# Loading a small vector last on SyncE's queue instead of first on ScalarE's

## The chip, the core and the metric

The kernel runs on one core of a Trainium2 chip. The core has a matrix engine (TensorE, "PE" in the profile, with its weight loads shown apart as "PEld"), a vector engine (VectorE, "DVE"), a scalar engine (ScalarE, "ACT"), GpSimd ("POOL") and SyncE ("SP"), which here only issues DMAs. ScalarE issues a few DMAs too. Every engine works through its own list of instructions in order, and waits on semaphores for what others produce. The metric is the device time of one execution in microseconds (us); what is compared is the median of several executions.

## What is computed

The reference is a state-space convolution block followed by a two-layer network. Shortened:

```python
# q, k, v: (1, 2048, 512) bf16; shift_k: (512, 4); ssm_k: (512, 2048); ssm_D: (512,)
k_shift = sum over t of k_pad[:, t:t + S, :] * shift_k[:, ks - 1 - t]
kv  = k_shift * v
y   = irfft(rfft(kv, 2 * S) * rfft(ssm_k, 2 * S))[:S] + kv * ssm_D    # along the sequence
h   = x + layernorm(x) * y                                            # x is q
out = h + relu(layernorm(h) @ w1) @ w2
```

What matters for this change is ssm_D, 512 numbers of 2 bytes. Since kv * ssm_D is the convolution of kv with a single tap at position 0, the kernel adds ssm_D to the real part of the spectrum of ssm_k, and needs nothing more of it.

## The kernel before

All is written for one core and these sizes, with the order of the instructions on each engine fixed by the order in the program text.

**Loads.** `wsh` (the four shift taps) is loaded on ScalarE's queue at L95. Right behind it, on the same queue, two loads bring ssm_D (L102, tile `d0`, in the trace "d"): one for each half of the 64 + 64 partitions. Each writes the same 64 columns of four row groups to all 64 partitions, so that each half is 64 partitions of 4 runs of 64 numbers, 32 KB. On SyncE's queue follow nine loads in this order: k of the first 512 tokens (a DMA transpose, L125, tile `kT`), all of ssm_k (a plain load of 2 MB, L122, into the tile `pre`), v of the first 512 tokens (a DMA transpose, L127, tiles `vT`), and then k and v in turns for the other three quarters. SyncE's next instruction after these is the load of x at L405, which can only start when the memory of the middle stage is free.

**First stage, to about 38 us.** TensorE runs eleven warm-up matmuls (L115), then the taps of the first quarter: `taps(u)` multiplies k by diagonal matrices (L273, tile `pkv` in PSUM), and `times_v(u)` on VectorE multiplies the result by v (L280, tile `kvx`). When ssm_k is there, 64 transposes (L219) bring it into rows, and eight groups of `stage1` (L246, copied out by ScalarE and VectorE at L233 and L235) make the first half of its spectrum. The taps of the later quarters stand between these groups.

**GpSimd in this stage.** It makes the negated table `cn` from `cs` in eight pieces (L211, in the trace "c2n"). Between the first and the second piece it copies ssm_D into the order in which it is used (L213, tile `dtab`, from "d"). It then clears `dre` and `dim` (L300, L301), and fills them by eight small operations from `dsc` ("dm_f" in the trace, L318). `dre` and `dim` are the matrices of the inverse transform at L455, which runs from about 94 us.

**Second stage, from about 38 us.** `kvx` is brought into rows (L219 again, tile `xfl`). Then the pool `early` is closed, which holds `d0`, `dsc`, `kvx` and some tables, and a pool is opened in its place which holds `kf`. `spectrum_k` makes the second half of the spectrum of ssm_k: matmuls (L261, L263, tile `ps2k`), then VectorE adds `dtab` to the real part on the way from PSUM to `kf` (L336), and ScalarE copies the imaginary part (L337). The first L336 is the first to need `dtab`, and the first to write over the memory of `early`.

**Later stages** (products, inverse transform, layer norms, the two-layer network and the stores, L367 to L596) use nothing of what is moved, but for `dre` and `dim`.

Of the kernel before, what the change touches and what calls it, by code (L numbers as in the profile page):

```python
# [15 lines left out]
P = 128  # L16
# [40 lines left out]
def kernel(  # L57
# [13 lines left out]
    nc = tc.nc  # L71
# [5 lines left out]
    DC = D // P  # L77
# [19 lines left out]
    pre = slotA.tile([P, 4096 + 2048], I32, tag="A", name="pre")  # L97
    skf = pre[:, 0:4096].bitcast(BF16)
    d0 = early.tile([P, DC, 64], BF16, name="d0")
    for dp in range(2):  # L100
        src = bass.AP(tensor=A_ssm_D.tensor, offset=A_ssm_D.offset + 64 * dp, ap=[[0, 64], [P, DC], [1, 64]])
        nc.scalar.dma_start(out=d0[64 * dp:64 * dp + 64, :, :], in_=src)  # L102
    CH = 512
    vTs = [vp.tile([P, DC, CH], BF16, name=f"vT{c}") for c in range(4)]
    kT = kvp.tile([P, DC, 16 + S], BF16, name="kT")
# [13 lines left out]
    for c, src in ((0, "k"), (0, "s"), (0, "v"), (1, "k"), (1, "v"), (2, "k"), (2, "v"), (3, "k"), (3, "v")):  # L119
        ts = slice(CH * c, CH * c + CH)  # L120
        if src == "s":
            nc.sync.dma_start(out=skf.rearrange("p (c t) -> p c t", c=DC),  # L122
                              in_=A_ssm_k.rearrange("(c p) t -> p c t", p=P))
        elif src == "k":
            nc.sync.dma_start_transpose(out=kT[:, :, 16 + CH * c:16 + CH * c + CH], in_=k_d[ts, :])  # L125
        else:
            nc.sync.dma_start_transpose(out=vTs[c][:], in_=v_d[ts, :])  # L127


    TURN = 2.0 * math.pi * SIN_SHRINK  # L130
# [46 lines left out]
    def table(dst, turns, dps=(0, 1)):  # L177
        for dp in dps:
            nc.scalar.activation(out=dst[:, :, 64 * dp:64 * dp + 64], in_=turns, func=ACT.Sin,  # L179
                                 scale=hsc[:, dp:dp + 1], bias=hbi[:, dp:dp + 1])  # L180
# [27 lines left out]
    dtab = consts.tile([P, 8, DC, 8], BF16, name="dtab")  # L208
    for h in range(8):
        hs = slice(4 * h, 4 * h + 4)  # L210
        nc.gpsimd.tensor_single_scalar(out=cn[:, hs, :], in_=cs[:, hs, :].bitcast(F32), scalar=-1.0, op=ALU.mult)  # L211
        if h == 0:
            nc.gpsimd.tensor_copy(out=dtab[:], in_=d0[:].rearrange("p r (o g) -> p o r g", g=8))  # L213


    def to_rows(cols, q, fl, eng):
# [52 lines left out]
    def taps(u):  # L269
        c, rg = divmod(u, DC)  # L270
        ps = psum.tile([P, CH], F32, tag="ps", name="pkv")
        for j in range(KS):
            nc.tensor.matmul(out=ps[:], lhsT=wdiag[:, rg, j, :], rhs=kT[:, rg, CH * c + 16 - j:CH * c + CH + 16 - j],  # L273
                             start=(j == 0), stop=(j == KS - 1))
        return u, ps

    def times_v(u, ps):
        c, rg = divmod(u, DC)
        split = "p (a h l) -> p a h l"
        nc.vector.tensor_tensor(out=kvx[:, :, rg, 8 * c:8 * c + 8, :].rearrange("p h a l -> p a h l"),  # L280
                                in0=ps[:].rearrange(split, h=16, l=4),
                                in1=vTs[c][:, rg, :].rearrange(split, h=16, l=4), op=ALU.mult)

    def group_k(gb):
        stage1(gb, kfl, lambda o, j, n: a1k[:, :, 32 * o + j:32 * o + j + n], "AADAAADA")
# [22 lines left out]
    for gb in range(8):  # L308
        for u in ((4, 5), (6,), (7,), (8, 9), (10, 11), (12,), (13, 14), (15,))[gb]:
            times_v(*taps(u))  # L310
        group_k(gb)
        if 2 <= gb < 6:

            hs = slice(8 * gb - 16, 8 * gb - 8)
            table(cc[:, hs], r2[:, hs], (1,))
    for pq in halves:
        for dst, rho, blk, sgn in ((dre, 0, 0, 1.0), (dre, 1, 1, 1.0), (dim, 0, 1, -1.0), (dim, 1, 0, 1.0)):
            nc.gpsimd.tensor_single_scalar(out=dst[pq, rho, pq], in_=dsc[pq, blk, :], scalar=sgn / 2048, op=ALU.mult)  # L318
# [367 lines left out]
```

## Time and profile before

| what | value |
|---|---|
| median of 5 executions | 218.05 us (217.62 to 219.07) |
| the profiled execution's own time | 219.07 us |
| its span in the trace | 217.3 us |
| mean granted clock of TensorE | 0.983 |
| ssm_D: two issues on ScalarE's queue, first and last start | 1.2 and 1.9 us |
| ssm_D: from issue to landing | 4.2 and 5.6 us |
| ssm_k: issue, time to landing | 2.19 us, 10.5 us |
| last issue of v on SyncE's queue: start, length, time to landing | 26.77 us, 2.30 us, 6.1 us |
| GpSimd: the eight operations of L318 | 26.27 to 29.35 us |
| first use of `dtab` (L336) | 42.58 us |

The span is the time from the first to the last instruction in the trace; the execution's own time is a little longer. Engines overlap, so their busy times don't add up to the span. Rows for a group of instructions give the engine, the operation, what is written and read, how many there are, how long they were busy, and what ended the idle time of the engine before them. For a DMA, "landing" is when its semaphore has been counted up, and "ACTq" and "SPq" are the engines that issue it; an issue takes the engine some time of its own. "q1" is the queue of SyncE's loads, "q10" that of ScalarE's, "q8" that by which instructions are loaded. The names of tiles lack their numbers.

### The profile page before, as it was taken

What the parts mean: (1) busy time and instruction counts of PE and PEld (TensorE: products, weight loads), DVE (VectorE), ACT (ScalarE), POOL (GpSimd) and SP (SyncE); (2) the same over time, 40 slices, a digit from 0 to 9 for tenths busy, and PEclk for the clock granted to TensorE, in tenths of its full rate; (3) what the DMA queues carried; (4) which work ended last, traced back from release to release, by engine and by line L of the source; (5) the groups of instructions that cost most, each with busy time, mean ns of one, the idle gap of its engine ahead of it and who ended that gap; (6) DMA issues with size and microseconds to landing.
All of it is one profiled execution on the core that took longest, in us unless ns stands there. A gap on an engine that the chain in (4) does not pass through costs nothing.

```text
span 217.3 us, 7312 instructions
## 1 busy us (share of the span) xinstructions
PE 204.3 (94%) x3129; PEld 141.4 (65%) x3129; DVE 147.2 (68%) x300; ACT 125.8 (58%) x240; POOL 67.7 (31%) x103
## 2 busy tenths in 40 slices
PE   7969888999999999999986999999999999999993
PEld 2466444999989999979973778554454544444442
DVE  6976877989989998867977779742973167130032
ACT  2485797798888888868935389103650337106500
POOL 6049930000019999978221120210022002000000
PEclk9999999999999999999998599999999999999999
DMA  6999980000000000049990000332124110621012
GB/s 129 354 200 147 186 165 8 0 8 3 3 3 3 2 3 0 0 113 223 278 298 4 6 3 0 51 69 55 27 50 63 39 50 0 91 73 32 0 42 54
DMA packets 30383, 15.40 MB, mean 71 GB/s; under 512 B 25520, under 2 KB 29072, under 8 KB 30224
## 3 DMA queue, kind: packets, MB, share of 16 engines
q1 hardware_dynamic: 28992, 14.75, 31.1%
q8 instruction: 24, 0.39, 0.8%
q10 hardware_dynamic: 1360, 0.20, 0.6%
q14 instruction: 7, 0.06, 0.1%
HBM read 7.08 MB, written 2.10 MB: 42 GB/s over the span
## 4 chain that ended last, share of the span: by engine, by line
PE 78%; SPq 6%; DVE 5%; DMA 3%; issue 3%; ACT 2%; DVEq 0%
PE ps2m L591 18%; PE ps1m L579 16%; PE pz L511 10%; PE psy L386 7%; SPq L127 4%; PE ps L246 4%; PE pkv L273 4%; PE psi L455 4%; PE u L261 4%; PE ps2k L261 4%; PE u L263 4%; DMA vT<-in_A_v_dram 3%; PE ps2k L263 3%; PE pst L219 2%; SPq L125 2%
## 5 line engine op out<-in xcount | busy, mean ns | idle before, releaser
L581 ACT ACTIVATE h1T<-ps1m 128x512 bf16<-128x512 f32 (+3 forms) x55 | 27.4, 514 | 25.9 <-PE ps1m L579 25.1
L579 PE MATMUL ps1m<-hlnT,w 128*128 128x512 bf16 (+3 forms) x220 | 39.6, 337 | 0.3
L591 PE MATMUL ps2m<-w,h1T 128*128 128x512 bf16 (+3 forms) x187 | 39.1, 367 | 0.0
L593 DVE TENSOR_TENSOR o<-ps2m,xh 128x512 bf16<-128x512 f32 (+1 forms) x17 | 11.1, 659 | 37.6 <-PE ps2m L591 37.1
L579 PEld LDWEIGHTS <-w 128*128 128x128 bf16 (+1 forms) x220 | 21.8, 100 | 17.6 <-issue 1.4
L591 PEld LDWEIGHTS <-h1T 128*128 128x128 bf16 (+1 forms) x187 | 17.9, 98 | 20.6 <-issue 1.6
L511 PE MATMUL pz<-bp,ecore 32*32 32x128 f32 x1024 | 22.2, 388 | 2.6 <-issue 2.0
L233 ACT CAST a<-ps 128x512 fp32r<-128x512 f32 x40 | 21.1, 593 | 4.4 <-PE ps L246 2.9
L525 POOL TENSOR_SCALAR rstd<-mv 128x4 f32<-128x4 f32 (+1 forms) x9 | 2.1, 230 | 67.2 <-DVE mv L532 61.3
L520 ACT CAST zt<-pz 128x512 bf16<-128x512 f32 x16 | 8.4, 596 | 24.6 <-PE pz L511 21.6
L511 PEld LDWEIGHTS pz<-bp,ecore 32*32 32x32 f32 x1024 | 15.6, 110 | 8.3 <-issue 4.6
L376 POOL TENSOR_TENSOR t<-usb,kf 128x320 fp32r<-128x320 f32 x22 | 19.7, 943 | 1.7 <-ACT usb L367 1.6
L376 DVE TENSOR_TENSOR t<-u,kf 128x704 fp32r<-128x704 f32 x22 | 18.4, 883 | 1.8 <-ACT usb L367 1.6
L233 ACT CAST kf<-psy 128x512 fp32r<-128x512 f32 x30 | 17.6, 647 | 1.9 <-PE psy L386 0.2
L530 DVE BATCH_NORM_STATS2 st<-xh 128x6 f32<-128x512 bf16 x28 | 17.3, 678 | 0.0
L235 DVE CAST a<-ps 128x512 fp32r<-128x512 f32 x24 | 15.8, 686 | 1.9 <-PE ps L246 1.8
L455 PE MATMUL psi<-dre,kf 128*128 128x256 f32 x64 | 15.2, 285 | 0.2 <-ACT kf L233 0.2
L273 PE MATMUL pkv<-kT,wdiag 128*128 128x512 bf16 x64 | 15.4, 381 | 0.0
L455 PE MATMUL psi<-dim,kf 128*128 128x256 f32 x64 | 15.1, 285 | 0.0
L211 POOL TENSOR_SCALAR c2n<-c2s 128x512 fp32r<-128x512 f32 x8 | 11.8, 1513 | 9.1 <-ACT c2s L179 9.1
L280 DVE TENSOR_TENSOR kvx<-pkv,vT 128x512 bf16<-128x512 f32 x16 | 10.5, 686 | 5.4 <-DMA vT<-in_A_v_dram 4.8
L455 PEld LDWEIGHTS psi<-dre,kf 128*128 128x128 f32 x64 | 12.1, 192 | 0.7 <-ACT kf L233 0.7
(119 smaller groups left out, 400.4 us busy)
## 6 DMA issues: line engine op xcount, KB each, us to landing
pre<-in_A_ssm_k_dram SPq DMA_DIRECT2D x1, 2048.0 KB, 10.5
out_dram<-o SPq DMA_DIRECT2D x58, 32.0 KB, 1.6
xh<-in_A_q_dram SPq DMA_DIRECT2D x4, 384.0 KB, 7.0
w<-in_B_w_dram SPq DMA_DIRECT2D x1, 1376.0 KB, 12.7
w<-in_B_w_dram SPq DMA_DIRECT2D x1, 1280.0 KB, 16.0
xh<-in_A_q_dram SPq DMA_DIRECT2D x4, 128.0 KB, 3.1
hlnT<-hln SPq DMA_TRANSPOSE x12, 3.1
w<-in_B_w_dram SPq DMA_DIRECT2D x1, 96.0 KB, 15.6
```

Of the source, the lines that this page charges most:

```text
L233: nc.scalar.copy(out=o, in_=i)
L235: nc.vector.tensor_copy(out=o, in_=i)
L261: nc.tensor.matmul(out=ps[:, kk, :], lhsT=w_re[:, k1, :], rhs=a_in(col(k1, 0)), start=True, stop=False, skip_group_check=True)
L273: nc.tensor.matmul(out=ps[:], lhsT=wdiag[:, rg, j, :], rhs=kT[:, rg, CH * c + 16 - j:CH * c + CH + 16 - j], start=(j == 0), stop=(j == KS ...
L376: eng.tensor_tensor(out=t[:, :, j, :], in0=in0.unsqueeze(1).to_broadcast([P, 2, n, 2]), in1=kfr[:, :, j, ks], op=ALU.mult)
L386: nc.tensor.matmul(out=psy[:], lhsT=m_[:], rhs=t_.rearrange("p j k -> p (j k)"), start=first, stop=not first)
L455: nc.tensor.matmul(out=ps, lhsT=kf[:, c, 4 * m:4 * m + 4, :].rearrange("p r k -> p (r k)"), rhs=(dre, dim)[c][:].rearrange("p a b -> p (a ...
L511: nc.tensor.matmul(out=pz[32 * a:32 * a + 32, r4, l4, :], lhsT=ecore[rows, rho, n2, :], rhs=rhs, start=(rho == 0), stop=(rho == 1), tile_p ...
L530: nc.vector.bn_stats(out=st[:, t % 4, :], in_=xh[:, t, :])
L579: nc.tensor.matmul(out=ps1[:fsz, :], lhsT=w1[:, c, fc * P:fc * P + fsz], rhs=hlnTs[sc][:, c, part], start=(c == 0), stop=(c == DC - 1))
L581: nc.scalar.activation(out=h1s[sc][:fsz, fc, part], in_=ps1[:fsz, :], func=ACT.Relu)
L591: nc.tensor.matmul(out=ps2[:], lhsT=h1s[sc][:ksz, fc, i * P:(i + 1) * P], rhs=w2[:ksz, fc, ds], start=(fc == 0), stop=(fc == NFC - 1))
```

## The change

The two loads of ssm_D leave ScalarE's queue, where they were issued after `wsh`, and are issued by SyncE after the nine loads of k, ssm_k and v. GpSimd's copy into `dtab` leaves its place between the pieces of the negated table, and stands right ahead of the eight operations that fill `dre` and `dim`. Sizes, shapes and the rest of the program are the same.

```diff
     d0 = early.tile([P, DC, 64], BF16, name="d0")
-    for dp in range(2):
-        src = bass.AP(tensor=A_ssm_D.tensor, offset=A_ssm_D.offset + 64 * dp, ap=[[0, 64], [P, DC], [1, 64]])
-        nc.scalar.dma_start(out=d0[64 * dp:64 * dp + 64, :, :], in_=src)
...
             nc.sync.dma_start_transpose(out=vTs[c][:], in_=v_d[ts, :])
+    for dp in range(2):
+        src = bass.AP(tensor=A_ssm_D.tensor, offset=A_ssm_D.offset + 64 * dp, ap=[[0, 64], [P, DC], [1, 64]])
+        nc.sync.dma_start(out=d0[64 * dp:64 * dp + 64, :, :], in_=src)
...
         nc.gpsimd.tensor_single_scalar(out=cn[:, hs, :], in_=cs[:, hs, :].bitcast(F32), scalar=-1.0, op=ALU.mult)
-        if h == 0:
-            nc.gpsimd.tensor_copy(out=dtab[:], in_=d0[:].rearrange("p r (o g) -> p o r g", g=8))
...
             table(cc[:, hs], r2[:, hs], (1,))
+    nc.gpsimd.tensor_copy(out=dtab[:], in_=d0[:].rearrange("p r (o g) -> p o r g", g=8))
     for pq in halves:
         for dst, rho, blk, sgn in ((dre, 0, 0, 1.0), (dre, 1, 1, 1.0), (dim, 0, 1, -1.0), (dim, 1, 0, 1.0)):
             nc.gpsimd.tensor_single_scalar(out=dst[pq, rho, pq], in_=dsc[pq, blk, :], scalar=sgn / 2048, op=ALU.mult)
```

## The prediction

> **What bounds the kernel now.** I read the page's first lines, then the chain of waits of the first 45 us, because all that the change touches lies there, then TensorE's waits in the same stretch.
>
> ```profile
> span 217.3 us, 7312 instructions
> PE 204.3 (94%) x3129; PEld 141.4 (65%) x3129; DVE 147.2 (68%) x300; ACT 125.8 (58%) x240; POOL 67.7 (31%) x103
> ...
> 2.19 0.73 SPq L122
> 2.98 9.46 SPq L127
> 12.48 2.14 SPq L125
> 14.66 7.10 DMA vT<-in_A_v_dram
> ...
> 31.79 1.53 issue
> 33.33 0.48 PE ps L246 x39
> ...
> PE pst L219 <- DMA pre<-in_A_ssm_k_dram: 1.9, 1, 1.9
> PE ps L246 <- issue: 1.5, 1, 1.5
> ```
>
> The chain's columns are start, length and what ran. TensorE is busy for 94% of the span, so a change pays only where TensorE stops. Up to 22 us the chain is not TensorE at all: it is SyncE issuing the loads (ssm_k at L122, the transposes of k at L125 and of v at L127) and then the second v load, landing at 21.76. TensorE stops three times on account of loads: 1.9 us until ssm_k lands (2.19 + 10.5 = 12.7), then about 1.2 us near 22 us until VectorE has that v, then 1.53 us at 31.79. After 33.33 it works nearly without a gap to 94 us. So time taken out of the loads before 12.7 us reaches the end, and time added after 33 us reaches it only if TensorE is made to stop.
>
> The 1.53 us needs a closer look. TensorE stops after 25 weight loads of a group of 64 (L246) and goes on at 33.33, while the VectorE operation that follows the last v load still runs (32.99 to 33.68); so it waited for no PSUM bank of that operation. In the DMA view of 30 to 31 us one packet of the instruction queue starts where the transposes' packets run out, about 30.65, and takes 7.3% of 16 engine-microseconds, 1.17 us on its one engine:
>
> ```profile
> q1 hardware_dynamic: 771, 0.19, 85.3%
> q8 instruction: 1, 0.02, 7.3%
> ```
>
> (queue, packets, MB, share). I read the stop as TensorE waiting for its next block of instructions, which came late because the transposes of v held the DMA engine. Here a rule and a row differ. The Trainium skill, "Runtime: NRT & Kernel Launch", section Instruction fetch mechanics, says that instructions come in 16 KiB blocks fetched while the block before runs, and that crossing a boundary is mostly hidden. By the rule the 1.53 us would be something else, and no shift of loads could touch it; by the row it hangs on what the DMA engines do at 28 to 31 us. I go with the row, and it makes one of the rivals.
>
> **The change, part by part.** The lines for what is moved:
>
> ```profile
> L102 ACTq DMA_DIRECT2D d<-in_A_ssm_D_dram x2: 651/667/683, 1.2 to 1.9; - x2
> L213 POOL COPY dtab<-d x1: 411/411/411, 15.2 to 15.2; 128x256 bf16<-128x256 bf16 x1
> ...
> DMA to landing us min/median/max: 4.2/4.9/5.6
> ...
> 2.58 1.28 ACT L145 ACT_TABLE_LOAD   x1 [2.58 <-issue]
> 5.89 0.32 ACT L145 ACTIVATE f_f<-f_t,nbias 128x32 f32<-128x32 int32 x1 [2.03 <-DVE f_t L46]
> ...
> q1 hardware_dynamic: 1524, 0.65, 87.7%
> q10 hardware_dynamic: 522, 0.06, 13.7%
> ...
> 28.55 0.80 POOL L318 TENSOR_SCALAR dim<-dm_f 64x64 fp32r<-64x64 f32 x2
> ...
> 42.58 1.35 DVE L336 TENSOR_TENSOR kf<-ps2k,dtab 128x512 fp32r<-128x512 f32 x2
> ...
> SPq L405 <- DVE t L376: 63.7, 1, 63.7
> ```
>
> 1. ScalarE loses two issues of 0.67 us, so its table load starts 1.3 us sooner. Worth nothing: its first activation waited 2.03 us for VectorE's f_t. The load of wsh, ahead of them, stays.
>
> 2. ssm_D's packets leave the start. The two queue lines above are 3 to 6 us: 522 packets on ScalarE's queue (q10), 13.7% of 3 us, which is 0.41 us of every DMA engine. They ran beside the end of the first k and the start of ssm_k. The first k gains nothing: TensorE begins on it at 5.66, when its eleven warm-up matmuls end. ssm_k can gain. Upper end 0.41 us, if every engine was full. Lower end 0, if the packets fitted into holes; from 4.5 to 7 us the two queues filled 76.8% + 7.2% = 84%. Is ssm_k's slow start the neighbour's doing, which would be worth more? It moved 0.57 MB in those 2.5 us; the loads of x at 94.9 to 97.4 us, with no such neighbour, moved 0.50 MB. So it starts slowly by itself and I add nothing. I take 0.84 x 0.41 = 0.34, rounded to 0.3 us (an estimate). Nothing is put in ahead of 29 us, so this term is not below 0 by itself. The gain goes through: ssm_k lands earlier, the first v issue (9.46 us, held until ssm_k was nearly drained) ends earlier, and so do all later transposes and TensorE's stops behind them. **-0.3 us.**
>
> 3. SyncE gets two issues behind the last v issue (26.77 + 2.30 = 29.07). The nearest row for a plain load issued right behind a transpose is ssm_k's, 0.73 us; with 0.67 to 0.73 each they end at about 30.5. Upper end: held like the first v, 9.46 us (rival D). Behind them on SyncE is only L405, the load of x, at 94.37, after a wait of 63.7 us for VectorE: 0. On the DMA engines they stand behind the last v on the same queue, so v is not delayed; from 31 to 94 us there is next to no other load.
>
> 4. ssm_D lands, with 5.6 us from 30.5, by 36.1 at the latest. A rule speaks against this move: the Trainium skill, "DMA: Bandwidth & Descriptors", Rules for kernel authors, advises issuing a DMA early and waiting on it late. Before, it lay ready some 8 us ahead of the copy; now GpSimd waits. The same page's fixed cost (Anatomy of one DMA) of some 2 us, stated for GpSimd's path, would have it there by about 32.6; the rows say 4.2 to 5.6, and I use them. Either way it is before the need.
>
> 5. GpSimd: the copy (0.41 us) leaves 15.16, so seven negations and the memsets come 0.4 us sooner; their reader, the c2n matmul, is at 42.0, so 0. The copy now stands ahead of the eight L318 operations (26.27 to 29.35, 3.08 us) and holds them: copy to 36.5, L318 to 39.6. Their matmuls come at 94 us. But kf lies in the memory of the pool that holds d0 and dm_f, so L336 at 42.58 waits for copy and L318: slack 42.6 - 39.6 = 3.0 us. Cost 0; without this cover each late microsecond would cost VectorE one. GpSimd now works beside VectorE at 36 to 39.6 instead of 26 to 29; L280 took 0.69 us with and without GpSimd at work, so 0 again.
>
> **Sum.** -0.3. The profiled execution took 219.07, 1.77 around its span of 217.3; it would become 217.0 and 218.8. It was the slowest of the five shown, 1.0 above the median; against the median, 218.05 - 0.3 = 217.75, say **217.7 us**.
>
> **The rivals.**
>
> A, the forecast: 217.7, chance 0.58, own range 217.1 to 218.4.
>
> B: the instruction block slips into an earlier gap. The third k's packets run out at about 28.5; had the block gone there and not at 30.65, TensorE would not have stopped at 31.79, and the last k, 1.2 us later, would still be in time (landing 29.4 + 1.2 = 30.6, needed at 33.8). That gives 218.05 - 0.3 - 1.5 = 216.2. For it: the gaps are narrow, and a shift of tenths can decide. Against it: TensorE and the loads both move with ssm_k. Chance 0.17. The profiled run being slow may mean that other executions already have it.
>
> C: the packets sat in holes anyway, 218.05. For it, the engines at 84% and a slow start without them. Chance 0.13.
>
> D, slower: SyncE's issues are held behind what is ahead of them, as the first v was. The first starts when the last v has landed (32.9), lands 0.7 + 5.6 later (39.2), the second the same after it (45.5). Copy and L318 end at 49.0, the first L336 at 49.7, and TensorE, with eight PSUM banks filled by 44.3, stops for 5.4 us: 218.05 - 0.3 + 5.4 = 223.1. It decides once ssm_D lands after about 40.1 (43.6, when L336 must start, less 0.41 and 3.08), 11 us after 29.07. Against it: ssm_k's issue was not held behind a transpose. Chance 0.08.
>
> The last 0.04: the instruction block falls later, slower by more than a microsecond.
>
> **How the numbers follow.** This kernel's measurement can tell about 0.5%, 1.1 us, from no change. A (but for 0.03) and C lie within it: 0.68. Faster: B and that tail of A, 0.20. Slower: D and the last case, 0.12. The range 216.1 to 218.8 holds A, B and C and leaves D and the last case out.
>
> **What would show it.** Step 2: ssm_k landing at 12.3 to 12.5 and TensorE's wait 0.2 to 0.4 us shorter. Step 3: two issues of about 0.7 us after 29 us. Step 4: landing by 36. Step 5: L318 ending before 40 and no wait ahead of L336. Rival B: no gap in L246 near 31.5. Wrong would be a wait of VectorE or TensorE on dtab at 42 us, or ssm_k landing over 0.5 us earlier.

## The result, and the profile after

The changed kernel took 217.71 us in the median (43 runs) against 217.87 (80 runs) for the kernel before. The ratio is 0.9986 with a 95% interval of 0.9973 to 0.9999, so the gain is 0.14%, or 0.3 us, and somewhere between 0.02 and 0.6 us; the two medians themselves lie 0.16 us apart. Ratios here leave out executions that took over 1.5% longer than the fastest of their kernel: one of these 43, and five of the 22 behind the 0.9968 of the first run without a load below, which by plain means of all 22 would be about 0.998. The gain is within the 0.5% that was set as the bound of "no change", and the forecast was 217.7.

The two profiled executions suggest something else: the span fell from 217.3 to 215.5 us, six times as much. So the first lesson is in reading the profile after with care. Its first lines, the chain of waits of the first 45 us (start, length, what ran), and TensorE's waits in that stretch:

```profile
span 215.5 us, 7313 instructions
...
2.19 10.26 DMA pre<-in_A_ssm_k_dram
12.49 5.90 PE pst L217 x64
...
30.55 0.97 issue
31.52 0.48 PE ps L244 x39
...
PE pst L217 <- DMA pre<-in_A_ssm_k_dram: 1.8, 1, 1.8
PE ps L244 <- issue: 1.0, 1, 1.0
```

All of the 1.8 us is gone before 32 us: TensorE's group L244 goes on at 31.52 where it went on at 33.33. Three places make it up. ssm_k lands at 12.45 instead of 12.68 (0.2 us). The stop near 22 us, where TensorE waited for VectorE and VectorE for the second v, is not there any more (about 1.0 us; the first line below is that wait in the kernel before). The stop at the instruction block is 0.97 instead of 1.53 us (0.6 us). From there on the two traces keep their distance.

First two lines of the kernel before: TensorE's wait near 22 us, and SyncE's queue in 4.5 to 7 us (queue, packets, MB, share of the 16 engines). Then the lines of what was moved, in the changed kernel: ssm_D's issues and copy, GpSimd's operations behind it, the first L335 (L336 before), and the same stretch of SyncE's queue:

```profile
PE ps L246 <- DVE kvx L280: 0.9, 2, 0.5
q1 hardware_dynamic: 162, 0.57, 76.8%
```

```profile
L127 SPq DMA_DIRECT2D d<-in_A_ssm_D_dram x2: 605/666/728, 28.0 to 28.7; - x2
L314 POOL COPY dtab<-d x1: 396/396/396, 32.5 to 32.5; 128x256 bf16<-128x256 bf16 x1
...
DMA to landing us min/median/max: 3.7/3.9/4.2
...
35.16 0.80 POOL L317 TENSOR_SCALAR dim<-dm_f 64x64 fp32r<-64x64 f32 x2
...
40.76 1.41 DVE L335 TENSOR_TENSOR kf<-ps2k,dtab 128x512 fp32r<-128x512 f32 x2
...
q1 hardware_dynamic: 187, 0.77, 88.7%
```

The late side went as forecast: two issues of 0.67 us from 28.0, ssm_D there at 32.4 and copied at 32.5, GpSimd done at 35.96, and L335 starts at 40.76 with nothing to wait for, 4.8 us later. The early side has a surprise in its last line: 0.77 MB of ssm_k had gone by 7 us, against 0.57 before.

### The profile page after: what moved, and what is told of

Its sections match the earlier page's. It is cut to its first block, busy times and chain, and to the rows that moved or that the text cites. A ratio compares the mean times of both kernels' runs of the same rounds, so it can differ in the third digit from the quotient of the medians.

```text
span 215.5 us, 7313 instructions
## 1 busy us (share of the span) xinstructions
PE 204.0 (95%) x3129; PEld 140.8 (65%) x3129; DVE 147.0 (68%) x300; ACT 125.8 (58%) x240; POOL 67.7 (31%) x103
## 4 chain that ended last, share of the span: by engine, by line
PE 84%; DVE 5%; DMA 5%; ACT 2%; issue 2%; SPq 1%
PE ps2m L590 18%; PE ps1m L578 16%; PE pz L510 10%; PE psy L385 7%; PE pkv L271 5%; DMA pre<-in_A_ssm_k_dram 5%; PE ps L244 5%; PE pst L217 4%; PE psi L454 4%; PE u L259 4%; PE ps2k L259 4%; PE u L261 4%; PE ps2k L261 3%; DVE bp L233 2%; DVE a L233 1%
## 5 line engine op out<-in xcount | busy, mean ns | idle before, releaser
L278 DVE TENSOR_TENSOR kvx<-pkv,vT 128x512 bf16<-128x512 f32 x16 | 10.5, 685 | 4.3 <-DMA vT<-in_A_v_dram 2.2
## 6 DMA issues: line engine op xcount, KB each, us to landing
pre<-in_A_ssm_k_dram SPq DMA_DIRECT2D x1, 2048.0 KB, 10.3
w<-in_B_w_dram SPq DMA_DIRECT2D x1, 1280.0 KB, 15.6
```

## The experiments

The theory: ssm_D's packets, taken from the start, are worth the 0.3 us, and the late place is free. The rivals: GpSimd's new order is what pays; the queue (a compute engine's) is what pays; the late place costs something that hides a larger gain. The experiments ran in three groups, each beside the kernel before on the same chip. Ratios are to the kernel before.

**One part alone: GpSimd's copy moved, the loads left where they were.**

```diff
-        if h == 0:
-            nc.gpsimd.tensor_copy(out=dtab[:], in_=d0[:].rearrange("p r (o g) -> p o r g", g=8))
...
+    nc.gpsimd.tensor_copy(out=dtab[:], in_=d0[:].rearrange("p r (o g) -> p o r g", g=8))
     for pq in halves:
```

> The kernel before with one part of the change: GpSimd's copy into dtab stands ahead of the eight operations that fill dre and dim, while both loads of ssm_D stay first on ScalarE's queue. If the 0.3 us come from the packets that left the start (my theory), this kernel equals the one before: ratio 1.000, within 0.1%. If they come from GpSimd's new order (the negated table ready 0.4 us sooner), it is faster by 0.3 us like the whole change: 0.9986.

Measured: 0.9998 (0.9979 to 1.0017). The order on GpSimd gives nothing that shows, though the interval would still allow the 0.3 us. As far as the loads go, this run is also a second execution of the kernel before, and its profile is telling: its span is 215.6 us, as short as that of the changed kernel. TensorE's waits in its first 50 us:

```profile
PE pst L217 <- DMA pre<-in_A_ssm_k_dram: 1.1, 1, 1.1
PE ps L244 <- issue: 0.9, 1, 0.9
PE ps L244 <- DVE kvx L278: 0.3, 1, 0.3
```

The stop near 22 us (the last line) is 0.3 us here and was 0.9 in the first profile; the stop at the block is 0.9 and was 1.5. With the loads in the same place, single executions differ by more than the change is worth.

**The changed kernel again**, twice, beside other runs.

> The changed kernel itself once more, as the standard for the runs beside it: 0.9986 against the kernel before, within 0.2%. Its profile is a second execution of the same program: if the 1.8 us between the two spans shown are mostly the luck of one execution, its wait for ssm_k, its stop near 22 us and its stop at the instruction block differ from those of the first by several tenths of a microsecond each.

> The changed kernel a third time, as the standard for the two runs beside it: 0.998 to 0.999 of the kernel before.

Measured: 0.9984 (0.9964 to 1.0005) and 0.9978 (0.9955 to 1.0). The second lies just below what was expected of it. With the first result that is three times a gain of 0.14 to 0.22%, though the intervals of these two reach no change. Their spans were 214.8 and 215.7 us, and ssm_k took 10.0 and 10.5 us to land. Of the three places named for the second execution, only the wait for ssm_k differed by several tenths (1.2 against 1.8 us); the stop near 22 us was absent again, and the stop at the block took 0.9 against 1.0 us. So the landing of ssm_k, which I had named as the sign of the gain, varies by 0.5 us from one execution to the next.

**No load at all.** The changed kernel, with the tile of ssm_D filled with zeros.

```diff
-    for dp in range(2):
-        src = bass.AP(tensor=A_ssm_D.tensor, offset=A_ssm_D.offset + 64 * dp, ap=[[0, 64], [P, DC], [1, 64]])
-        nc.sync.dma_start(out=d0[64 * dp:64 * dp + 64, :, :], in_=src)
+    nc.gpsimd.memset(d0[:], 0.0)
```

> The changed kernel without the two loads of ssm_D: GpSimd fills the tile with zeros instead, so the term kv * ssm_D is missing from the output; the copy into dtab stays where the change put it. If the loads cost nothing at their new place, this equals the changed kernel: 0.9986 against the kernel before, ssm_k landing at 12.4 to 12.5. If the late loads take something (from the last v, or from the instruction block that is fetched near them), it is faster than that: 0.995 to 0.997. If ssm_D's packets never cost anything, it is 1.000.

> The changed kernel without the two loads of ssm_D (zeros in their tile, the term kv * ssm_D missing) once more, now beside the changed kernel on the same chip. If the late loads are free, the two agree within 0.15%. If the 0.18% between 0.9968 and 0.9986 is real, this one is again faster than the changed kernel by 0.4 us.

Measured: 0.9968 (0.9946 to 0.9989), then 0.9992 (0.9975 to 1.0009) beside the changed kernel's 0.9978. The first looked as if the late loads cost 0.4 us; the second takes that back. The two average 0.998, like the changed kernel's three. At its new place ssm_D costs nothing that can be measured here; the two pairs differ by 0.18% one way and 0.14% the other.

**More packets early.** Two more loads of 128-byte runs right behind ssm_D's (four times as many packets), then four more (eight times as many).

```diff
         nc.scalar.dma_start(out=d0[64 * dp:64 * dp + 64, :, :], in_=src)
+    dx = early.tile([P, 16, 80], BF16, name="dx")
+    for dp in range(2):
+        src = bass.AP(tensor=A_shift_k.tensor, offset=A_shift_k.offset, ap=[[0, 64], [64, 16], [1, 64]])
+        nc.scalar.dma_start(out=dx[64 * dp:64 * dp + 64, :, 0:64], in_=src)
```

> The kernel before with two more loads right behind those of ssm_D on ScalarE's queue, into a tile that nobody reads: again 128-byte runs, four times as many packets (2048), so five times the early packets in all, 1.64 us more of each DMA engine. If a packet ahead of ssm_k delays it by 0.84 of its own time, as the prediction has it, ssm_k lands 1.4 us later and the kernel takes 1.4 us more (1.006). If ssm_D's packets went into holes and the true rate is that of the whole change (0.3 us for 0.41 us, 0.73), 1.2 us more. If small packets cost nothing there, 1.000.

> The kernel before with four more loads behind those of ssm_D on ScalarE's queue, eight times as many packets (4096 more, 3.3 us more of each DMA engine). The run with half of them cost 0.2%, 0.44 us, or 0.27 us per microsecond of packets. If that rate holds, this one costs 0.9 us: 1.004. If the prediction's 0.84 were right and the run before an outlier, 2.8 us: 1.013. If the packets are hidden until they hold ssm_k, there is a bend: under 0.2% or well over 0.4%.

Measured: 1.002 (1.0001 to 1.004), that is 0.44 us, and 1.0171 (1.0126 to 1.0216), 3.7 us. Neither is the test that it was meant to be, of packets ahead of ssm_k. The extra loads were issued from 2.62 us, ssm_k at 2.19, and their packets came late. ScalarE's queue (q10) in 3 to 6, 9 to 12 and 12 to 15 us of the run with two more loads:

```profile
q10 hardware_dynamic: 521, 0.06, 13.5%
...
q10 hardware_dynamic: 525, 0.07, 31.8%
...
q10 hardware_dynamic: 1463, 0.18, 44.7%
```

The 521 of the start are those of the kernel before (522 there), ssm_D's own. From 6 to 9 us there were only 115, then 525 beside the end of ssm_k, and most came from 12 us on, about or after its landing at 12.9 us, beside the transposes of v and k. So the 0.44 us are not the price of early packets, and the prediction's 0.84 was not tested. In the run with four more loads most of the packets came late too, and it has a bend for another reason. ScalarE's queue (start, length, engine, line, what) and a wait of VectorE in that run:

```profile
2.62 11.59 ACTq L107 DMA_DIRECT2D dx<-in_A_shift_k_dram  x4
14.25 1.28 ACT L150 ACT_TABLE_LOAD   x1 [14.25 <-issue]
...
DVE f_hi L204 <- ACT f_f L150: 6.8, 1, 6.8
```

Four issues took 11.6 us instead of some 2.7. The third alone took 6.6 us and the fourth 3.6, until 14.2 us, when ssm_k had landed (13.4). ScalarE works in order, so its table load and first activations came at 14 us and later (its table load began at 4.0 us in the run with two more loads), VectorE waited 6.8 us for them, and TensorE, halfway through the rows of ssm_k, another 3.0 for VectorE. In the run with two more loads the issues took 1.37 us and nothing was held. So this run prices above all a held compute engine, with a later ssm_k and later transposes besides, and no rate per packet follows from either run.

What the early packets do to the start is seen best side by side (to landing, and MB on SyncE's queue in 4.5 to 7 us):

| kernel | ssm_D's place | first k lands after | MB, 4.5 to 7 us | ssm_k lands after |
|---|---|---|---|---|
| before | early | 4.8 us | 0.57 | 10.5 us |
| copy moved only | early | 4.7 us | 0.59 | 10.3 us |
| two more loads | early, the other packets later | 4.5 us | 0.57 | 10.7 us |
| changed | late | 4.2 us | 0.77 | 10.3 us |
| changed, second | late | 4.2 us | 0.72 | 10.0 us |
| changed, third | late | 4.1 us | 0.85 | 10.5 us |
| no load, second | none | 4.1 us | 0.75 | 10.1 us |

Columns three and four separate cleanly: without the packets, the first k lands about half a microsecond sooner and some 0.15 to 0.3 MB more of ssm_k has gone by 7 us. The four other traces whose start is that of the changed kernel (late on ScalarE's queue, more packets late, and the two runs at the end) fall in with them: 4.1 to 4.3 us, 0.79 to 0.82 MB. The last column doesn't separate: these four landed after 10.1 to 10.5 us, so the means are 10.4 (before and copy moved) and 10.3 (eight without the packets), and the spread is far larger than the difference. Most of the head start is gone in the tail of the load: of the 4,096 packets of ssm_k only 15 were left after 10.5 us in the changed kernel's trace and 48 in that of the kernel before, and yet it landed just 0.2 us sooner.

**Late, but on ScalarE's queue.**

```diff
-    for dp in range(2):
-        src = bass.AP(tensor=A_ssm_D.tensor, offset=A_ssm_D.offset + 64 * dp, ap=[[0, 64], [P, DC], [1, 64]])
-        nc.sync.dma_start(out=d0[64 * dp:64 * dp + 64, :, :], in_=src)
...
     table(cc, r2[:], (0,))
+    for dp in range(2):
+        src = bass.AP(tensor=A_ssm_D.tensor, offset=A_ssm_D.offset + 64 * dp, ap=[[0, 64], [P, DC], [1, 64]])
+        nc.scalar.dma_start(out=d0[64 * dp:64 * dp + 64, :, :], in_=src)
```

> The changed kernel with the two loads of ssm_D issued by ScalarE after its third large table (L179, about 15.6 us) instead of by SyncE behind the last v: late, but on ScalarE's queue. If only the packets' leaving of the start counts (my theory), it comes near the changed kernel, with two small debts: ScalarE spends 1.3 us on issues where it had 0.9 us to spare, and the packets run beside a k and v pair: 0.9986 to 1.001. If the queue is what counts (ScalarE is a compute engine, and an issue there can be held[...], as in the run with four more loads, where four issues took 11.6 us), ScalarE is held for several microseconds while ssm_k's rows wait in PSUM: 1.004 or more.

Measured: 1.0003 (0.9981 to 1.0025), in the range of the first theory; ScalarE was not held (0.71 and 0.61 us an issue). The issues fell at 12.6 and 14.7 us, sooner than the 15.6 expected and far ahead of the late place on SyncE's queue, so this run changes queue and place together. The start was as quick as in the changed kernel (first k after 4.1 us), but here the packets run beside k and v, and in its trace TensorE waited for VectorE near 22 us again, VectorE for the second v:

```profile
PE ps L244 <- DVE kvx L278: 1.1, 2, 0.7
```

The ratio lies near no change, and its interval holds the changed kernel's gain too. Being off the start alone was not shown to pay.

**More packets late.** Two more loads, like those above, behind ssm_D's on SyncE's queue.

```diff
         nc.sync.dma_start(out=d0[64 * dp:64 * dp + 64, :, :], in_=src)
+    dx = early.tile([P, 16, 80], BF16, name="dx")
+    for dp in range(2):
+        src = bass.AP(tensor=A_shift_k.tensor, offset=A_shift_k.offset, ap=[[0, 64], [64, 16], [1, 64]])
+        nc.sync.dma_start(out=dx[64 * dp:64 * dp + 64, :, 0:64], in_=src)
```

> The changed kernel with two more loads behind those of ssm_D on SyncE's queue, 128-byte runs into a tile that nobody reads, four times as many packets. If the late place is free (my theory), the ratio is that of the changed kernel, 0.9986. If the late loads cost what the kernel without any load seemed to save beyond the change (0.9986 - 0.9968 = 0.0018, 0.4 us), four times as many packets cost some 1.6 us more: about 1.006.

Measured: 1.000 (0.9972 to 1.0028), beside 0.9984 for the changed kernel; the intervals overlap, and 1.006 is excluded. Its trace shows a second stop of TensorE, at 36 us, in the eighth group of stage 1 (weight loads from the first stop on, with the idle time before each row in brackets):

```profile
31.98 0.37 PEld L248 LDWEIGHTS <-kfl 32*128 32x128 bf16 x39 [1.38 <-issue]
32.39 1.41 PEld L275 LDWEIGHTS <-wdiag 128*128 128x128 bf16 x8
34.23 0.57 PEld L248 LDWEIGHTS <-kfl 32*128 32x128 bf16 x64 [0.42 <-issue]
34.84 0.55 PEld L275 LDWEIGHTS <-wdiag 128*128 128x128 bf16 x4
35.81 0.17 PEld L248 LDWEIGHTS <-kfl 32*128 32x128 bf16 x13 [0.42 <-issue]
37.08 0.47 PEld L248 LDWEIGHTS <-kfl 32*128 32x128 bf16 x51 [1.10 <-issue]
```

No other trace has a stop there. It is likely that the added loads made it, and that the place behind the last v is not free without end, but one trace doesn't show it. Between the two stops lie 39 + 8 + 64 + 4 + 13 = 128 weight loads, each with its matmul: 256 instructions. The next experiment says what such stops are.

**The stop at the instruction block.**

```diff
     first = [taps(u) for u in range(4)]
-    warm_up(7)
+    warm_up(3)
+    for _ in range(36):
+        nc.tensor.matmul(out=warm[:, 0:64], lhsT=wz[:, 0:P], rhs=wz[:, 0:64], start=True, stop=True)
```

> The changed kernel with 64 more TensorE instructions in the wait for ssm_k: four of the seven warm-up matmuls there are replaced by 36 small ones (64 columns instead of 512). If TensorE's stop near 31 us is a wait for the next 256 instructions, it moves by exactly 64 instructions to an earlier place: from behind the 25th of the 64 weight loads of the sixth group of stage 1 to near the end of the fifth group. If the stop belongs to data (a PSUM bank, the last v), it stays where it was. The time is left open between 0.995 and 1.003, since the block is then asked for at another moment of the transposes.

Measured: 1.011 (1.0067 to 1.0153), slower than expected. The weight loads of the changed kernel first, then those of this one:

```profile
29.20 0.55 PEld L271 LDWEIGHTS <-wdiag 128*128 128x128 bf16 x4
30.17 0.26 PEld L244 LDWEIGHTS <-kfl 32*128 32x128 bf16 x25 [0.42 <-issue]
31.51 0.37 PEld L244 LDWEIGHTS <-kfl 32*128 32x128 bf16 x39 [1.09 <-issue]
```

```profile
28.89 0.55 PEld L244 LDWEIGHTS <-kfl 32*128 32x128 bf16 x61 [0.42 <-issue]
31.85 0.11 PEld L244 LDWEIGHTS <-kfl 32*128 32x128 bf16 x3 [2.41 <-issue]
```

The stop went from behind the 25th load of the sixth group to behind the 61st of the fifth. In between lie 3 loads, the 4 of the taps and 25 more: 32 pairs of weight load and matmul, 64 instructions, exactly those put in. No wait for data would count instructions. Counted from the start of the program, the stop stands behind the 479th weight load in all twelve traces that have it, this one included.

The instruction queue shows where the wait comes from. Its packets are 16,384 bytes for 256 instructions. In these twelve traces the packet for this boundary starts 2.4 to 3.1 us after TensorE passed the boundary before, while the transposes run, and TensorE goes on 1.2 to 1.6 us after the packet's end. Once they have passed this boundary, the next packet starts 1.0 to 1.8 us later, and TensorE does not stop at the next one; only in the run with more packets late it starts 2.8 us later, and there is the second stop. In the run with ScalarE held, the packet for the boundary of the 479th load started after 1.1 us, and TensorE did not stop.

The stop also grew here from 1.1 to 2.4 us, and another of 0.4 us came at 26.5 us, 128 weight loads ahead. The growth and this stop make about two thirds of what this kernel loses against the changed one (0.0124 of 217.5, 2.7 us); the rest was not traced to a place.

**How late may the late side be?** Six more operations on GpSimd between the copy and the eight behind it.

```diff
+    gx = early.tile([P, 4, P], F32, name="gx")
...
     nc.gpsimd.tensor_copy(out=dtab[:], in_=d0[:].rearrange("p r (o g) -> p o r g", g=8))
+    for _ in range(6):
+        nc.gpsimd.tensor_single_scalar(out=gx[:], in_=cs[:, 0:4, :].bitcast(F32), scalar=-1.0, op=ALU.mult)
     for pq in halves:
```

> The changed kernel with six GpSimd operations of 1.5 us (into a tile that nobody reads) between the copy into dtab and the eight operations behind it, which then end about 45 us instead of 36. If kf's memory is held by these eight operations, the first L335 waits from 40.8 to about 45, TensorE's filled PSUM banks cover about 1.0 us of it, and the kernel is some 3 us slower than the changed one (ratio to the kernel before about 1.013). If only the copy itself counts, nothing changes: 0.9986.

Measured: 1.0232 (1.0186 to 1.0277), more than the 1.013 expected. GpSimd's last operation, then VectorE's and TensorE's waits:

```profile
45.80 0.80 POOL L320 TENSOR_SCALAR dim<-dm_f 64x64 fp32r<-64x64 f32 x2
...
DVE kf L338 <- POOL dim L320: 5.8, 1, 5.8
...
PE ps2k L260 <- ACT kf L339: 5.0, 1, 5.0
```

VectorE waits for the eight operations, though it needs nothing of what they write: they read from the memory that kf takes over. They ended at 46.6 and not at 45, TensorE's filled PSUM banks covered 0.8 of the 5.8 us, and TensorE stood still for 5.0. That is nearly the whole of the loss against the changed kernel (0.0246 of 217.5, 5.4 us).

## Why the prediction was right, point by point

The sum was right: -0.3 us forecast, 0.3 us measured, with an interval of 0.02 to 0.6. The late side (points 3 to 5) was right in its mechanism too. That the early side came out at just this size is luck as far as these runs show, for its path was not borne out (point 2).

1. ScalarE's two issues are worth nothing: nothing contradicts it. The run with ScalarE held shows what the slack was worth: issues that are not held lie under the wait for f_t, held ones cost microseconds.

2. The packets at the start: the size came out right and its working did not. I said that ssm_k "starts slowly by itself" and put nothing down to the neighbour. The table shows the neighbour: 0.57 to 0.59 MB with ssm_D's packets, 0.72 to 0.85 without. The comparison with the loads of x, which have another shape, misled me; its window also opens 0.4 us ahead of the first packet of x. In turn I took ssm_k's landing to gain what its packets gain, 0.84 of 0.41 us; the landings show 0.1 to 0.2 us in the mean, inside their spread. The rate of 0.84 was tested by no run, since the packets that were added came after ssm_k's. And the run that was off the start, but on ScalarE's queue, had the quick start without a gain that shows. Where the measured gain comes from is thus not settled. A candidate is the second v: TensorE's wait for VectorE near 22 us was 0.9, 0.3 and 0.2 us in the three profiles with ssm_D's packets at the start (the third is that with two more loads), absent in all three of the changed kernel and in three of four other runs with the same quick start, and 0.2 us in the fourth (the six extra operations). With the packets beside k and v, on ScalarE's queue, it was 1.1 us. That is a pattern and no proof; no run holds the second v alone. That the first k gains nothing in time was right: it landed 0.5 us sooner, under the warm-up matmuls.

3. SyncE's two issues: 1.38 us together, nothing behind them. Right. In one later trace, that of the six extra operations, the second issue took 1.7 us.

4. Landing: by 32.4 us, where 36.1 was the latest that I allowed. The rows (4.2 to 5.6 us) were too pessimistic for the quiet place; 3.7 and 4.2 were measured. The rule that speaks against the move, to issue early, had no say here: 4.8 us of slack were left at L335.

5. GpSimd: that the copy and the eight operations hold kf was right, shown by the six extra operations. They sized rival D too: TensorE stands still for what lies beyond the slack and some 0.8 us of cover, 5.0 us in that run.

Of the rivals, D did not happen: the issues were not held behind v. B was right in its mechanism and wrong in its hope. The stop is a wait for an instruction block, shown by the 64 instructions, and the block comes late while the transposes run, as the prediction read it; so the rule that crossing a block is mostly hidden does not hold in this stage. But the change doesn't move the stop: 1.5 and 0.9 us before (the copy alone counted as before), 1.0, 0.9 and 1.3 after. C, no gain, is excluded only just, by the first result alone. The profiled run's 219.07 us, which I suspected of being slow by a stop, was indeed the luck of one execution.

## What to carry to other kernels

A change of tenths of a microsecond cannot be read from two profiles: the spans here differed by 1.8 us, the medians of many runs by 0.2. Compare several executions of each, stop by stop, and let the times of many executions side by side decide. Before an experiment is read as a price, look at when its packets ran: loads issued 0.4 us behind ssm_k had most of theirs 10 us later. A small load is safe where no transfer is in a hurry and no compute engine issues it. And a quicker start of a large load need not reach its landing: here 0.15 to 0.3 MB of head start became 0.1 to 0.2 us. When something moves late, look not only for who reads it, but for whose memory is freed by what stands behind it.

## What was not expected of the hardware

An issue on ScalarE's queue can hold ScalarE itself: four small loads issued from 2.6 us took 11.6 us behind a 2 MB load, while two took 1.37. TensorE stopped at a boundary of its instruction blocks, near 31 us, in every trace but that of the held ScalarE, for about 0.7 to 1.5 us, and for 2.4 us when the boundary lay 64 instructions earlier. The blocks are 256 instructions. The packet that brings this one started 2.4 to 3.1 us after TensorE had entered the block before it, and took 0.9 to 1.2 us. And a queue's packets can run long after the issue: those of two small loads on ScalarE's queue, issued at 2.6 and 3.3 us, came mostly after the 2 MB load issued just ahead of them, and landed 11.4 to 12.3 us after their issue.
